# The end of batch 1's attention: masks of the last head pair on TensorE, its heads in one run, x of two pairs transposed by DMA, an earlier Gelu table load

## Chip, cores and metric

The kernel runs on 1 core of one Trainium2 chip. The time is the device time of one execution in microseconds; the figure for a kernel is the median of its runs.

## The reference

Attention with a forget gate over 8 batches and 8 heads, 576 tokens, head size 64, followed by a two-layer network with an exact Gelu on all 4608 tokens:

```
scores = q @ k.T / sqrt(64);  cum = cumsum(log(clip(f, 1e-4, 1)))
attn   = softmax(where(causal, scores + cum[i] - cum[j]))
x      = (attn @ v) with heads side by side: [4608, 512]
out    = gelu(x @ w_in) @ w_out          # w_in 512x2048, w_out 2048x512
```

All inputs and the output are float32; the kernel multiplies in bf16.

## The kernel before, in words

The work goes batch by batch, in an order that is written out by hand (`tc.manual_schedule()`): each engine executes its instructions in the order in which the code issues them. The engines are called PE (TensorE), DVE (VectorE), ACT (ScalarE), POOL (GpSimd) and SP (SyncE, which issues DMAs).

The 8 heads of a batch are 4 pairs. For a pair `i`, `scores(b, i, t)` (L280) computes one of four tiles `t` of transposed scores for both heads into PSUM (pool `s_psum`, two buffers), keys on the partitions and queries along the free dimension; ACT takes the exp into `e` (L310). Only blocks on or below the diagonal are computed. The diagonal blocks need the causal mask, and this is done in one of two ways: where `on_pe` is true (L281), PE adds a large negative number by small matmuls of the constants `key_of` and `after` ahead of the exp; elsewhere POOL sets the forbidden entries of `e` to zero by `affine_select` behind the exp (L312). Per pair there are five such diagonal blocks.

`attend` (L324) multiplies e with the weighted v (`vw`, the factor of the forget gate and a column of sums in it) into the PSUM tile `o` (pool `o_psum`, two buffers); `normalize` (L339) has DVE take the reciprocal of the sums and write x (bf16, tag `x`, three buffers). x has tokens on the partitions; the first GEMM wants it transposed, as xT. There are two ways for that too: `to_xT` (L357) transposes on PE through PSUM and copies by DVE or ACT, and `x_dma` (L369) has SP issue one DMA that transposes through the DMA crossbar. Batches 2 to 7 use `x_dma`, batches 0 and 1 `to_xT`.

Then `gemm1` (L381) makes 16 blocks of the hidden layer for the first 512 tokens of the batch (the last 64 are gathered in `tails` for one pass at the end), and ACT's Gelu follows each (L406). The second GEMM of a batch is used as filler: it is a generator from which `take(fill, n)` takes n matmuls in the gaps of the next batch's attention. For batch 1 the filler is `gemm2_first` (L510), half of batch 0's second GEMM: 16 matmuls of 128x512 at L518, into two buffers of `m_psum`, which DVE copies out at the 12th step and ACT at the 16th (L530).

`second_attention` (L721) is batch 1. Its order for the pairs: `tiles(i, t)` issues two score tiles, `run(i)` attends to and normalizes both heads of a pair. At the end come the transposes of x of pairs 0 and 1 by PE (`o_psum` buffers, DVE copies), pair 2 (into `s_psum`, ACT copy), and pair 3 inside `gemm1_begin` (L642), which starts the first GEMM with two blocks on the parts of x that are there (`m_psum`, the two buffers that the filler leaves). Between them SP issues `transpose_dma(2, ...)` (L226), the crossbar transposes of q and k of batch 2, as soon as POOL's loads of them have landed, and after that `load_v(2)`. DVE sorts the transposed q and k in `untangle` (L241). POOL waits for k (`behind`, L570) and issues two loads of w_out.

ACT keeps one table of functions at a time; a change between Exp and Gelu shows as ACT_TABLE_LOAD. A copy runs with either. A tiny activation on `warm` (L735) loads Exp's table ahead of batch 1's attention.

Of the kernel before, what the change touches and what calls it, by code (L numbers as in the profile page):

```python
# [11 lines left out]
Act = mybir.ActivationFunctionType  # L12
# [7 lines left out]
HP = 4  # L20
# [33 lines left out]
def kernel(  # L54
# [10 lines left out]
    nc = tc.nc  # L65
# [24 lines left out]
    o_psum = ctx.enter_context(tc.tile_pool(name="o_psum", bufs=2, space=PSUM))  # L90
# [40 lines left out]
    warm = consts.tile([P, TC], BF16)  # L131
# [42 lines left out]
    def load_w_out(c):  # L174
        kt = slice(c * n_ff // 4, (c + 1) * n_ff // 4)
        nc.gpsimd.dma_start(w_out_sb[:, kt, :], w_out_r[:, kt, :])
# [82 lines left out]
    def vw(b):  # L259
        if b not in vw_of:  # L260
            vw_of[b] = v_pool.tile([P, H, NBLK, D + 1], BF16, tag="vw", name=f"vw{b}")
        return vw_of[b]

    def weigh_v(b, i, eng=nc.gpsimd):

        hs = slice(2 * i, 2 * i + 2)
        bh = b * H + 2 * i
        w = wT[:, :, bh : bh + 2].rearrange("p n h -> p h n")
        eng.tensor_tensor(  # L269
            vw(b)[:, hs, :, 0:D],  # L270
            v_sb[:, hs, :, :],
            w.unsqueeze(3).to_broadcast([P, 2, NBLK, D]),
            Alu.mult,
        )
        if b:
            eng.tensor_copy(vw(b)[:, hs, :, D], w)
# [1 line left out]
    e_of = {}  # L278

    def scores(b, i, t):  # L280
        on_pe = b == 0 or (b == 1 and i == 0)  # L281
        st = s_psum.tile([P, 2, 512], FP32, tag="s", name=f"s{t}")
        c = 0
        for n, q0, w in STILES[t]:
            z = D if n == NBLK - 1 else 0
            masked = on_pe and c in SDIAG[t]
            for half in range(-1, 2 if masked else 0):
                if half == 0 and z:
                    continue
                for h in range(2):  # L290
                    d = slice(h * D, (h + 1) * D)
                    if half < 0:
                        to = st[:, h, c + z : c + w]
                        ab = kT[i][d, K0[n] : K0[n] + P], qT[i][d, q0 + z : q0 + w]
                    else:
                        last = (half + 1) * D
                        to = st[:, h, c + z : c + last]
                        c0 = (1 + h - half) * D
                        ab = key_of[d, c0 : c0 + P], after[d, c0 + z : c0 + last]
                    nc.tensor.matmul(  # L300
                        to, *ab, start=half < 0, stop=half == 1 or not masked
                    )
            c += w
        z = D if t == 1 else 0
        if z:
            et = e4[(b * HP + i) % len(e4)]
        else:
            et = e_pool.tile([P, 2, 512], BF16, tag=f"e{t}", name=f"e{t}")
        e_of[b, i, t] = et
        nc.scalar.activation(et[:, :, z:c], st[:, :, z:c], Act.Exp, scale=scale)  # L310
        for c0 in [] if on_pe else SDIAG[t]:
            nc.gpsimd.affine_select(  # L312
                out=et[:, :, c0 + z : c0 + P],
                in_=et[:, :, c0 + z : c0 + P],
                compare_op=Alu.is_ge,
                fill=0.0,
                base=z,
                pattern=[[0, 2], [1, P - z]],
                channel_multiplier=-1,
            )  # L320
# [3 lines left out]
    def attend(b, i, h, ms):  # L324
        if (b, i, h) not in o_of:
            o_of[b, i, h] = o_psum.tile([P, NBLK, D + 1], FP32, tag="o", name="o")
        o = o_of[b, i, h]
        for m in ms:
            for n in range(m + 1):
                t, c = where(n, m)  # L330
                nc.tensor.matmul(  # L331
                    o[:, m, :],
                    e_of[b, i, t][:, h, c : c + P],
                    vw_of[b][:, 2 * i + h, n, :],
                    start=(n == 0),
                    stop=(n == m),
                )

    def normalize(b, i, h):  # L339
        if (b, i) not in x_of:  # L340
            x_of[b, i] = x_pool.tile([P, NBLK, 2, D], BF16, tag="x", name="x")
        o = o_of[b, i, h]
        r = x_pool.tile([P, NBLK], FP32, tag="r", name="r")
        nc.vector.reciprocal(r, o[:, :, D])  # L344
        nc.vector.tensor_tensor(  # L345
            x_of[b, i][:, :, h, :],
            o[:, :, 0:D],
            r.unsqueeze(2).to_broadcast([P, NBLK, D]),
            Alu.mult,
        )  # L350

    def xT(b):
        if b not in xT_of:
            xT_of[b] = xT_pool.tile([P, n_dm, XC], BF16, tag="xT", name="xT")
        return xT_of[b]

    def to_xT(b, i, copy, pool=m_psum, tag="m", ps=None):  # L357
        if ps is None:
            shape = [P, 2, 1024] if pool is s_psum else [P, XC]
            ps = pool.tile(shape, BF16, tag=tag, name="ps_x")  # L360
            if pool is s_psum:
                ps = ps[:, 0, 0:XC]
        for m in range(NBLK):
            nc.tensor.transpose(  # L364
                ps[:, m * P : (m + 1) * P], x_of[b, i][:, m, :, :], ident_bf
            )
        copy(xT(b)[:, i, :], ps)

    def x_dma(b, i):  # L369
        nc.sync.dma_start_transpose(  # L370
            xT(b)[:, i, :].rearrange("d (m p) -> d m p", p=P),
            x_of[b, i].rearrange("p m h d -> p (m h d)"),
        )
# [136 lines left out]
    def gemm2_first(c):  # L510

        pss = [
            m_psum.tile([P, d_model], FP32, tag="m", name="ps2") for _ in range(2)
        ]
        for kq in (0, 4):
            for ts in range(2):
                for kt in range(kq, kq + 4):
                    nc.tensor.matmul(  # L518
                        pss[ts],
                        g_of[c][kt][:, ts * P : (ts + 1) * P],  # L520
                        w_out_sb[:, kt, :],
                        start=(kt == 0),
                        stop=(kt == 7),
                    )
                    if kt == 7:
                        ot_of.append(
                            o_pool.tile([P, d_model], FP32, tag="ot", name="ot")
                        )
                        copy = nc.scalar.copy if ts else nc.vector.tensor_copy
                        copy(ot_of[ts], pss[ts])  # L530
                    yield
# [27 lines left out]
    def take(gen, n):  # L559
        for _ in range(n):  # L560
            if next(gen, "end") == "end":
                return
# [7 lines left out]
    def behind(t, h):  # L570

        g = x_pool.tile([P, 1], FP32, tag="gate", name="gate")
        nc.gpsimd.tensor_copy(g[:PT], t[:, h, 0:1])
# [147 lines left out]
    def second_attention():  # L721


        b, fill = 1, gemm2_first(0)

        def av(i, h):
            attend(b, i, h, (0, 1, 2, 3, 4))
            normalize(b, i, h)

        def transposes(i, pool, tag):  # L730
            for which in range(2):
                transposes_first(b, i, which, pool, tag)


        nc.scalar.activation(warm[0:1, 0:1], warm[0:1, 0:1], Act.Exp)  # L735
        def tiles(i, t):
            scores(b, i, t)
            scores(b, i, t + 1)

        def run(i):  # L740
            av(i, 0)
            av(i, 1)

        tiles(0, 0)
        transposes(1, o_psum, "o")
        transposes(2, m_psum, "m")
        transposes(3, o_psum, "o")
        tiles(0, 2)
        take(fill, 2)
        tiles(1, 0)  # L750
        run(0)
        tiles(1, 2)
        take(fill, 4)
        weigh_v(1, 2)
        tiles(2, 0)
        run(1)
        weigh_v(1, 3)
        tiles(2, 2)
        take(fill, 4)
        tiles(3, 0)  # L760
        transpose_dma(2, 0, 4)
        transpose_dma(2, 4, 8)
        to_xT(b, 0, nc.vector.tensor_copy, o_psum, "o")
        to_xT(b, 1, nc.vector.tensor_copy, o_psum, "o")
        take(fill, 2)
        tiles(3, 2)
        behind(qk_of[2][1], H - 1)
        load_w_out(2)
        load_w_out(3)
        run(2)  # L770
        take(fill, 4)
        av(3, 0)
        both = s_psum.tile([P, 2, 1024], BF16, tag="s", name="ps_x2")
        to_xT(b, 2, nc.scalar.copy, ps=both[:, 0, 0:XC])
        av(3, 1)
        gemm1_begin(1, both)
        x_tail(1)
        load_v(2)
# [67 lines left out]
```

## Time and profile before

| what | value |
|---|---|
| median of 10 runs | 338.18 us (337.06 to 340.92) |
| the profiled execution, its own time | 337.12 us |
| its span in the profile | 335.3 us |
| granted TensorE clock, mean | 0.998 |
| exp (L310) | 128 activations, 100.2 us |
| POOL select (L312) | 135, 49.1 us, mean 383 ns |
| transposes of x on PE (L364) | 40, first at 21.2, last at 56.7 us |
| DMA, x to xT (L370) | 24, first at 84.0 us |

Times in the profile are microseconds from the start of the span. A timeline row gives the start, the time until the end of the last instruction merged into the row, the engine, the line of the kernel, the operation with its operands (written <- read), how many were merged, and in brackets the idle time ahead of it with what ended it. Matmuls are pipelined: the next starts before the last one's end, so the difference of starts is what one takes of PE. A few per cent of the matmul records are missing.

### The profile page before, as it was taken

The page shows a single profiled execution, that of the slowest core. Times are in us where ns is not written, and L with a number is a line of the kernel's source. Part 1 is how long each engine was busy: PE and PEld are TensorE (multiplying, and loading weights), DVE is VectorE, ACT ScalarE, POOL GpSimd, SP SyncE. Part 2 cuts the span into 40 slices and gives each one's busy share as a digit, 9 for nine tenths or more (in the row PEclk, how much of TensorE's full clock was granted, in tenths as well). Part 3 has the DMA queues.
Part 4 walks back from the last instruction along what each step waited for, and adds up shares of the span by engine and source line. Part 5 has one row for each costly group of instructions (what it writes and reads, how often), then busy time and mean ns, then how long its engine had stood idle before and what let it go on. Part 6 is the DMA issues. An engine that isn't in the chain of part 4 may idle for free.

```text
span 335.3 us, 7780 instructions
## 1 busy us (share of the span) xinstructions
PE 323.0 (96%) x3121; PEld 171.5 (51%) x3161; DVE 181.2 (54%) x414; ACT 209.3 (62%) x299; POOL 121.4 (36%) x250
## 2 busy tenths in 40 slices
PE   8799989999999999999999999999999999999995
PEld 3574556445554456445644555446544654444443
DVE  4770456674358945894579547964696550020011
ACT  6977797773634787378827892787378846404600
POOL 8280296037436144713445343624351420000000
PEclk9999999999999999999999999999999999999999
DMA  7999999979998999599947888689700241011013
GB/s 115 187 169 193 210 185 147 203 144 148 183 219 177 142 199 188 102 140 153 226 113 112 167 178 175 92 146 201 162 31 2 85 64 59 0 66 62 0 40 85
DMA packets 104627, 44.16 MB, mean 132 GB/s; under 512 B 83408, under 2 KB 100048, under 8 KB 104592
## 3 DMA queue, kind: packets, MB, share of 16 engines
q1 hardware_dynamic: 87296, 29.52, 46.7%
q0 software_dynamic: 16896, 13.63, 27.4%
q8 instruction: 24, 0.39, 0.5%
q10 hardware_dynamic: 400, 0.52, 0.4%
q14 instruction: 11, 0.09, 0.1%
HBM read 36.85 MB, written 9.44 MB: 138 GB/s over the span
## 4 chain that ended last, share of the span: by engine, by line
PE 90%; issue 2%; SPq 2%; DVE 1%; POOL 1%; ACT 1%; DMA 1%; POOLq 0%; ACTq 0%
PE ps L386 36%; PE ps L482 26%; PE o L331 10%; PE ps L422 8%; PE s L300 7%; SPq L120 2%; ACT e L310 1%; PE ps L542 1%; DMA v_sb<-in_v_dram 1%; POOL q L108 1%; PE ps_x L364 1%; PE ps L518 0%; POOL k L108 0%; DVE qT L217 0%; DVE kT L217 0%
## 5 line engine op out<-in xcount | busy, mean ns | idle before, releaser
L406 ACT ACTIVATE g<-ps 128x512 bf16<-128x512 f32 x144 | 82.1, 601 | 83.8 <-PE ps L386 83.8
L310 ACT ACTIVATE e<-s 128x896 bf16<-128x896 f32 (+2 forms) x128 | 100.2, 835 | 20.7 <-PE s L300 17.8
L386 PE MATMUL ps<-xT,w_in_sb 128*128 128x512 bf16 x497 | 111.7, 379 | 0.8
L482 PE MATMUL ps<-w_out_sb,g 64*128 64x512 bf16 (+1 forms) x692 | 104.4, 376 | 1.6 <-issue 1.3
L386 PEld LDWEIGHTS <-w_in_sb 128*128 128x128 bf16 x576 | 55.9, 98 | 67.7 <-issue 2.1
L312 POOL TENSOR_SCALAR_AFFINE_SELECT e<-e 128x256 bf16<-128x256 bf16 (+1 forms) x135 | 49.1, 383 | 84.7 <-ACT e L310 84.3
L482 PEld LDWEIGHTS <-g 64*128 64x128 bf16 (+1 forms) x711 | 39.4, 95 | 34.7 <-issue 4.2
L269 POOL TENSOR_TENSOR vw<-v_sb,wT 128x640 bf16<-128x640 f32 x30 | 38.6, 1289 | 27.3 <-PE s L300 14.3
L300 PE MATMUL s<-qT,kT 64*128 64x320 bf16 (+4 forms) x384 | 43.8, 276 | 2.8 <-ACT e L310 1.6
L250 DVE COPY kT<-tk 64x288 bf16<-64x288 bf16 x96 | 43.0, 448 | 1.6
L250 DVE COPY qT<-tq 64x288 bf16<-64x288 bf16 x96 | 39.8, 414 | 4.1 <-DMA tq<-q 2.7
L490 DVE COPY ot<-ps 128x512 f32<-128x512 f32 x20 | 13.8, 691 | 47.1 <-PE ps L482 47.1
L331 PEld LDWEIGHTS <-e 128*128 128x128 bf16 x960 | 34.5, 98 | 8.6 <-POOL e L312 2.5
L331 PE MATMUL o<-vw,e 128*128 128x65 bf16 x960 | 37.4, 194 | 1.3 <-issue 0.8
L345 DVE TENSOR_TENSOR x<-o,r 128x320 bf16<-128x320 f32 x64 | 31.4, 491 | 3.0 <-DMA xT<-x 0.8
L431 DVE COPY ot<-ps 128x512 f32<-128x512 f32 (+2 forms) x9 | 5.7, 632 | 49.6 <-PE ps L422 49.6
L300 PEld LDWEIGHTS <-kT 64*128 64x128 bf16 x384 | 19.8, 94 | 24.4 <-issue 7.9
L422 PE MATMUL ps<-w_out_sb,g 128*128 128x512 bf16 (+2 forms) x142 | 27.9, 355 | 0.1
L422 PEld LDWEIGHTS <-g 128*128 128x128 bf16 x144 | 13.5, 98 | 14.5
L344 DVE RECIPROCAL r<-o 128x5 f32<-128x5 f32 x64 | 12.1, 188 | 12.1 <-PE o L331 12.0
L502 DVE TENSOR_TENSOR ot<-ot,ps 128x512 f32<-128x512 f32 x22 | 15.1, 684 | 1.1
L386 PE MATMUL ps<-tails,w_in_sb 128*128 128x512 bf16 x63 | 14.2, 377 | 0.1
(69 smaller groups left out, 136.6 us busy)
## 6 DMA issues: line engine op xcount, KB each, us to landing
out_dram<-ot SPq DMA_DIRECT2D x32, 256.0 KB, 2.5
v_sb<-in_v_dram SPq DMA_DIRECT2D x24, 256.0 KB, 4.9
q<-in_q_dram POOLq DMA_DIRECT2D x6, 576.0 KB, 6.4
k<-in_k_dram POOLq DMA_DIRECT2D x6, 576.0 KB, 8.3
v_sb<-in_v_dram SPq DMA_DIRECT2D x22, 128.0 KB, 5.0
w_in_sb<-in_moe_w_in_dram POOLq DMA_DIRECT2D x4, 512.0 KB, 8.1
w_out_sb<-in_moe_w_out_dram POOLq DMA_DIRECT2D x4, 512.0 KB, 9.0
q<-in_q_dram POOLq DMA_DIRECT2D x4, 144.0 KB, 4.6
```

The source lines that it names most:

```text
L250: nc.vector.tensor_copy(rows[:, odd], src[odd * D : (odd + 1) * D, 2 * i + h].rearrange("d j p -> d p j"),)
L269: eng.tensor_tensor(vw(b)[:, hs, :, 0:D], v_sb[:, hs, :, :], w.unsqueeze(3).to_broadcast([P, 2, NBLK, D]), Alu.mult,)
L300: nc.tensor.matmul(to, *ab, start=half < 0, stop=half == 1 or not masked)
L310: nc.scalar.activation(et[:, :, z:c], st[:, :, z:c], Act.Exp, scale=scale)
L312: nc.gpsimd.affine_select(out=et[:, :, c0 + z : c0 + P], in_=et[:, :, c0 + z : c0 + P], compare_op=Alu.is_ge, fill=0.0, base=z, pattern=[[ ...
L331: nc.tensor.matmul(o[:, m, :], e_of[b, i, t][:, h, c : c + P], vw_of[b][:, 2 * i + h, n, :], start=(n == 0), stop=(n == m),)
L345: nc.vector.tensor_tensor(x_of[b, i][:, :, h, :], o[:, :, 0:D], r.unsqueeze(2).to_broadcast([P, NBLK, D]), Alu.mult,)
L386: nc.tensor.matmul(ps, w_in_sb[:, kt, ffb * P : (ffb + 1) * P], src[:, kt, 0:TC], start=(kt == 0), stop=(kt == n_dm - 1),)
L406: nc.scalar.activation(g_of[c][ffb], ps, Act.Gelu)
L422: nc.tensor.matmul(pss[ts][:, c0:c1], g_of[c][kt][:, ts * P : (ts + 1) * P], w_out_sb[:, kt, c0:c1], start=(kt == 0), stop=(kt == n_ff - 1),)
L482: nc.tensor.matmul(banks[r], g_of[c][kt][rows, ts * P : (ts + 1) * P], w_out_sb[rows, kt, :], start=kt == (steps.index("r") if r else 0), ...
L502: nc.vector.tensor_tensor(ot, ot, bank, Alu.add)
```

## The change

Four edits, all in batch 1. `scores` masks pair 3 (`HP - 1`) on PE as it does pair 0. x of pairs 0 and 1 goes to xT by `x_dma` right behind its `run`, in place of two `to_xT`. The two heads of pair 3 are issued in one `run(3)`, and the PE transposes of pair 2 follow it, where they lay between its heads; of the filler's last six matmuls four come ahead of the last two score tiles and two behind `run(2)`, where it was two and four. A tiny Gelu on `warm` is issued behind the last exp.

```diff
     def scores(b, i, t):
-        on_pe = b == 0 or (b == 1 and i == 0)
+        on_pe = b == 0 or (b == 1 and i in (0, HP - 1))
...
         run(0)
+        x_dma(b, 0)
         tiles(1, 2)
...
         run(1)
+        x_dma(b, 1)
         weigh_v(1, 3)
...
         transpose_dma(2, 0, 4)
         transpose_dma(2, 4, 8)
-        to_xT(b, 0, nc.vector.tensor_copy, o_psum, "o")
-        to_xT(b, 1, nc.vector.tensor_copy, o_psum, "o")
-        take(fill, 2)
+        take(fill, 4)
         tiles(3, 2)
+        nc.scalar.activation(warm[0:1, 0:1], warm[0:1, 0:1], Act.Gelu)
         behind(qk_of[2][1], H - 1)
         load_w_out(2)
         load_w_out(3)
         run(2)
-        take(fill, 4)
-        av(3, 0)
+        take(fill, 2)
+        run(3)
         both = s_psum.tile([P, 2, 1024], BF16, tag="s", name="ps_x2")
         to_xT(b, 2, nc.scalar.copy, ps=both[:, 0, 0:XC])
-        av(3, 1)
         gemm1_begin(1, both)
```

## The prediction

> **What bounds the kernel now.** I read the page's busy shares first, then the chain of work that ended last, then the timelines of PE, ACT, DVE, POOL and SP between 36 and 76 us, where batch 1's attention and what follows it lie, and last the rows of the DMA issues. The shares and the chain by engine:
>
> ```profile
> PE 323.0 (96%) x3121; PEld 171.5 (51%) x3161; DVE 181.2 (54%) x414; ACT 209.3 (62%) x299; POOL 121.4 (36%) x250
> PE 90%; issue 2%; SPq 2%; DVE 1%; POOL 1%; ACT 1%; DMA 1%; POOLq 0%; ACTq 0%
> ```
>
> PE is on the chain for 90% of the span, and from 57.44 us, where batch 1's first GEMM runs freely, the chain is PE nearly without a break. So the question is narrow: when does PE get to the matmul after the last `to_xT` of batch 1 (56.79 us now), and does anything later go late. PE around the change:
>
> ```profile
> 50.09 0.69 PE L300 MATMUL s<-qT,kT 64*128 64x256 bf16 x8
> 50.71 0.73 PE L364 MATMUL ps_x<-key_of,x 128*128 128x128 bf16 x10
> 51.28 0.59 PE L518 MATMUL ps<-w_out_sb,g 128*128 128x512 bf16 x2
> 51.80 0.74 PE L300 MATMUL s<-qT,kT 64*128 64x448 bf16 x4
> 52.47 1.12 PE L331 MATMUL o<-vw,e 128*128 128x65 bf16 x30
> 53.65 0.81 PE L518 MATMUL ps<-w_out_sb,g 128*128 128x512 bf16 x3
> 54.30 0.64 PE L331 MATMUL o<-vw,e 128*128 128x65 bf16 x15
> 54.77 0.44 PE L364 MATMUL ps_x<-key_of,x 128*128 128x128 bf16 x5
> 55.05 0.64 PE L331 MATMUL o<-vw,e 128*128 128x65 bf16 x15
> 55.53 1.02 PE L386 MATMUL ps<-xT,w_in_sb 128*128 128x512 bf16 x4
> 56.50 0.45 PE L364 MATMUL ps_x<-key_of,x 128*128 128x128 bf16 x5
> ```
>
> The reader is to use the starts: a duration contains about 0.16 us of pipeline that overlaps the next start. Ten transposes take 51.28 - 50.71 = 0.57 us of PE, five take 0.28, one fill matmul 0.215, a head of attention 0.48. One record of the fill is missing (16 weight loads, 13 matmuls over the stage), it lies at 53.43. PE stands still only near 50.3, 52.1 and 56.4, some 0.4 us together. ACT and SP beside it:
>
> ```profile
> 50.56 3.22 ACT L310 ACTIVATE e<-s 128x896 bf16<-128x896 f32 x4 [0.18 <-PE s L300]
> 54.50 0.58 ACT L530 COPY ot<-ps 128x512 f32<-128x512 f32 x1 [0.72 <-PE ps L518]
> 55.25 0.69 ACT L367 COPY xT<-ps_x 128x640 bf16<-128x640 bf16 x1 [0.17 <-PE ps_x L364]
> 55.96 1.28 ACT L406 ACT_TABLE_LOAD   x1
> 58.07 1.09 ACT L406 ACTIVATE g<-ps 128x512 bf16<-128x512 f32 x2 [0.83 <-PE ps L386]
> ```
>
> ```profile
> 50.91 1.41 SPq L236 DMA_TRANSPOSE tq<-q  x1
> 53.67 1.29 SPq L236 DMA_TRANSPOSE tk<-k  x1
> 55.01 2.33 SPq L236 DMA_TRANSPOSE tq<-q  x1
> 57.40 4.87 SPq L236 DMA_TRANSPOSE tk<-k  x1
> 62.36 4.09 SPq L120 DMA_DIRECT2D v_sb<-in_v_dram  x3
> ```
>
> Two things to see: after the table load ACT still waited 0.83 us for PE, so that load holds nobody up; and SP is free from 41.84 to 50.91.
>
> **The change, part by part.**
>
> *Masks by PE.* Pair 3 adds 18 small matmuls. Pair 0 of this batch shows their price:
>
> ```profile
> 38.67 0.25 PE L300 MATMUL s<-after,key_of 64*128 64x64 bf16 x4
> 38.76 0.25 PE L300 MATMUL s<-qT,kT 64*128 64x192 bf16 x2
> 42.08 0.26 PE L300 MATMUL s<-after,key_of 64*128 64x64 bf16 x4
> 42.27 0.39 PE L518 MATMUL ps<-w_out_sb,g 128*128 128x512 bf16 x1
> ```
>
> A group of four takes 0.09 us (38.67 to 38.76) up to 0.19 (42.08 to 42.27). Four groups and a pair of 0.02: between 0.4 and 0.8 us; I take 0.4, since the two groups inside a tile are the clean ones. Part of it hides: tile (3,1) waits until 50.44 for the exp of (2,3) anyhow, and tile (3,3) until 52.23 for the exp of (3,1). But the first tile's 0.17 us come before its exp, which had itself waited for PE (the 0.18 in brackets), so the four exps move from 50.56 to about 50.75.
>
> *Selects off POOL.* Five of 0.29 to 0.41 us go. The last ends at 54.26; PE needs its tile at 54.30, behind the fill. So this covers about itself: worth 0 now. But with only two fills after `run(2)`, the select would have held PE some 0.2 us; that is why the edits belong together. POOL also reaches the wait for k and the two w_out DMAs sooner, at k's landing.
>
> *Transposes of pairs 0 and 1.* PE is relieved of 0.57 us, DVE of two copies (0.89 us in all), which no one awaited closely. The bank order of the o pool changes: its two buffers go straight from pair 1 to pair 2.
>
> *Two x DMAs on SP.* They are issued when x is normalized, at 45.98 and 49.38 us, behind v loads whose issue ended at 41.84. SP's issue of one is 1.2 to 2.2 us (24 of them later), so the second ends at 50.6 to 51.6; the q transpose queued behind waited for its q data until 50.91, so it loses 0 to 0.7 us. Landing of an x DMA is 2.6 us at the least, 2.8 in the middle and 6.2 at most; the 6.2 is the one at 84.0 us, which ran under a bulk load of q and k, as these will. Lands: pair 0 by 52.2, pair 1 between 52.0 and 55.6. The first GEMM reads pair 1 in its second matmul, at about 55.8. Cost 0, just. Another reader of that landing: `normalize(3,0)` reuses x's first buffer and needs pair 0's DMA done by about 54.9; it has 2.7 us. A rule of the Trainium skill speaks to this ("DMA: Bandwidth & Descriptors", Queues, rings and completion order): an engine takes turns between queue rows, a packet at a time. A lone x DMA at 264 us used 0.82 us of all 16 engines and landed in 2.6; an even share with the software queue gives an estimate of 2.6 + 0.8 = 3.4 us. By the rule pair 1 lands at 52.8, by the worst row at 55.6; I take the row as the bound, and no stall by either.
>
> *What the DMAs delay.* The engines are full from 44 to 56.4 us, nearly idle from 56.5 to 57.5, full again to 71. Two x DMAs add 2 x 0.82 = 1.6 us; that gap takes up about 1.0. So the transposed q of heads 4 to 7, which DVE awaits until 65.66, comes 0.6 us later (0 to 1.6). DVE's untangling then ends at 71.7 instead of 71.06. Next for DVE is the sum at 72.07 (which waits 1.00 us for PE now), and the bank that it frees is wanted at 73.94, free at 73.48: slack 1.4 us in all. v lands near 72.3 for POOL's weighing; the selects that follow end at 78.4 and are read at 81.45, slack 3 us. Cost 0; at the bad end 0.2 us, or 0.8 if the gap absorbs nothing and SP also loses its 0.7.
>
> *Heads in one run, fill moved.* No matmul is added: two fills move ahead of tile (3,2), two stay between `run(2)` and `run(3)`. The cover between the heads of pair 2 and 3 shrinks from 0.87 us of fill to 0.43, and the five transposes between the heads of pair 3 go behind them. The o pool has two buffers, so head (3,1) needs (2,1) normalized. That was done at 54.50; here it moves with `run(2)`. Walk: exp (3,0) 50.75; four fills to 51.6; tile (3,2) at 51.7; exp (3,1) ends 52.38, tile (3,3) at 52.42; `run(2)` at 52.8 (was 52.47); fills from 53.75 to 54.2; (2,0) normalized 54.2, head (3,0) at 54.2 to 54.7; (2,1) normalized 54.8, head (3,1) at 54.85 to 55.35, a stall of 0.15; transposes of pair 2 to 55.6; first GEMM block to 56.5; its second `to_xT` at 56.5 (x of (3,1) is ready at 56.3), and 56.8 at the matmul after. Before it was 56.79: **0.0 us**. In a sum: -0.57 of transposes, +0.4 of masks, +0.15 on the o buffers.
>
> *Gelu's table sooner.* The load moves ahead of two ACT copies, behind the last exp at about 53.97. The tiny activation costs 0.11 to the next (40.20 to 40.31). The copy that frees the second m bank then runs 55.37 to 55.96, and PE asks for that bank at 56.04; the copy of pair 2 ends 56.65, asked for at 56.8. Both margins are 0.1 us, where 0.9 and 1.0 were before: a loss of 0 to 0.3 if ACT is a little later. Nothing is gained, since the Gelu waited for PE. The rule against it is the skill's "ScalarE: Activation LUTs", What ACT_TABLE_LOAD costs: 1283 ns and a drain of 1380 for each switch. The first number is the row's. A drain would push both copies by 1.38 us, and PE by about 1.3. The trace speaks against: the load at 38.91 begins within 0.03 us of the last Gelu's end (38.29 + 0.60) and the next activation starts at 40.20, 1.28 later plus 0.01. I take 1.28.
>
> **Sum.** Path 0.0 us, side costs nearer 0 than their ends. The profiled execution has a span of 335.3 us, 337.12 in its own time, so 1.8 lie around the span; the median of the ten runs is 338.18, 1.06 above that execution. I keep the difference and move the median by 0.0: 338.2 us.
>
> **The rivals.** A measurement of this kernel can tell about 0.5% (1.7 us) from no change.
> - *Even* (chance 0.62): as walked, 338.2, within 0.5 us.
> - *A small gain* (0.14): the masks hide fully in the waits at 50.44 and 52.23, and the o stall doesn't appear. Then -0.57, 337.6. For it: PE does stand there. Against: ACT's row of four exps starts later, and sets 52.23.
> - *A small loss* (0.13): masks at 0.8, ACT's copies late by 0.3, DVE late by 0.8: together up to +1.5, 339.7; typically +0.8, 339.0.
> - *The x DMA becomes the wait* (0.08), the other side: pair 1's x lands late and PE stands before the first GEMM. Decisive from a landing of 6.3 us, slower by the bound from 8.0. The transposed q issued at 55.01 took 10.6 us in a like crowd; that landing would put it at 60.0 and cost 4.2 us, 342.4. For it: the queue is full of q and k until 53.7. Against: the larger q transpose issued at 50.91, in the same crowd, took 3.9.
> - *Gain over the bound* (0.03): nothing on the path is that long (0.57 us of work and 0.4 of standing still); only the scatter of runs.
>
> Range: 337.2 (the small gain and 0.4 for scatter of medians) to 339.5 (most of the small loss). Chances with a share for scatter: faster 0.05, same 0.85, slower 0.10.
>
> **What would show it.** Right: 18 more masks in 50 to 53 us; no waits on xT's DMA at L386; two SP transposes at 46 and 49.4; the table load at about 54; Gelu still waiting for PE; the chain PE from 57 us. Wrong: PE idle before L386 released by a DMA or by the ACT copy of `ot`; DVE's untangling past 72.5; a start of the free-running GEMM more than 0.5 us off 57.4.

## The result, and the profile after

The changed kernel takes 339.69 us (median of 14 runs, 338.16 to 342.10), the kernel before 337.91 us in the runs beside it: ratio 1.0053, 95% interval 1.0033 to 1.0073. That is 1.8 us slower, outside the range of the prediction. The profiled execution took 339.49 us with a span of 337.2 us.

To see where, I cut each span at four points of PE's timeline that every kernel has: A, the first score matmul of batch 1's pair 3; B, the first matmul behind the last `to_xT` of batch 1; C, the first matmul of `gemm2_second` (L542); D, the first matmul of batch 2's first head (L331); E, the end.

| kernel | A | B - A | C - B | D - C | E - D | span |
|---|---|---|---|---|---|---|
| before | 50.09 | 6.70 | 13.35 | 11.31 | 253.85 | 335.3 |
| after | 50.43 | 7.89 | 13.35 | 12.01 | 253.52 | 337.2 |

Up to A the work is the same but for the two x DMAs, and from D it is the same; the differences of +0.34 and -0.33 are about as large as those among the kernels below that have no x DMA, and I take them as scatter. The loss lies in two places: 1.19 us between A and B, 0.70 us between C and D, together 1.9. The first lies in PE's timeline of the kernel after (to be held against the rows from 55.53 on before, which the prediction shows):

```profile
55.65 0.44 PE L364 MATMUL ps_x<-key_of,x 128*128 128x128 bf16 x5
56.81 1.29 PE L386 MATMUL ps<-xT,w_in_sb 128*128 128x512 bf16 x4 [0.72 <-DMA xT<-x]
58.03 0.45 PE L364 MATMUL ps_x<-key_of,x 128*128 128x128 bf16 x5
```

The transposes of pair 2 end near 55.93; the first GEMM then stands for pair 0's x DMA until 56.81, and its four matmuls take 1.22 us where they took 0.97 before: the second of them starts only at 57.29, when pair 1's x has come (57.2). The second place is in DVE's timeline, first a row of before, then four of after:

```profile
65.66 1.34 DVE L250 COPY qT<-tq 64x288 bf16<-64x288 bf16 x4 [2.66 <-DMA tq<-q]
```

```profile
56.86 0.49 DVE L345 TENSOR_TENSOR x<-o,r 128x320 bf16<-128x320 f32 x1 [1.44 <-DMA xT<-x]
69.28 1.35 DVE L250 COPY qT<-tq 64x288 bf16<-64x288 bf16 x4 [3.07 <-DMA tq<-q]
74.72 0.69 DVE L550 TENSOR_TENSOR ot<-ot,ps 128x512 f32<-128x512 f32 x1
75.44 0.69 DVE L502 TENSOR_TENSOR ot<-ot,ps 128x512 f32<-128x512 f32 x1
```

The first row of after is the x buffer that pair 0's DMA still has to read. In its second, the transposed q of heads 4 to 7 comes at 69.28 instead of 65.66, untangling ends at 74.7 instead of 71.1, and the sums that free the o bank follow without a gap, and PE takes the bank at 76.18 (before: 73.94, without a wait):

```profile
73.94 1.89 PE L482 MATMUL ps<-w_out_sb,g 64*128 64x512 bf16 x16
```

```profile
76.18 1.88 PE L482 MATMUL ps<-w_out_sb,g 64*128 64x512 bf16 x15 [0.33 <-DVE ot L502]
```

The chain of work that ended last, in order of time, tells the same story for the kernel after; before, it held ACT's exps and PE up to 53.65 us, and PE alone from there to the end of this stretch:

```profile
44.67 12.14 DMA k<-in_k_dram
56.83 1.40 SPq L236
58.28 10.97 DMA tq<-q
...
75.44 0.70 DVE ot L502
76.18 3.66 PE ps L482 x31
```

The load of batch 2's k took 12.14 us (9.3 before, 9.9 to 10.5 in those kernels below that have no DMA of x here), SP's transposes waited for it, and the transpose of q issued at 58.28 took 11 us.

### The profile page after: what moved, and what is told of

Its sections match the earlier page's. It is cut to its first block, busy times and chain, and to the rows that moved or that the text cites. A ratio compares the mean times of both kernels' runs of the same rounds, so it can differ in the third digit from the quotient of the medians.

```text
span 337.2 us, 7796 instructions
## 1 busy us (share of the span) xinstructions
PE 323.3 (96%) x3129; PEld 171.6 (51%) x3169; DVE 180.3 (53%) x412; ACT 209.4 (62%) x300; POOL 120.3 (36%) x245
## 4 chain that ended last, share of the span: by engine, by line
PE 82%; DMA 8%; DVE 3%; POOL 3%; SPq 2%; issue 2%; ACT 0%; POOLq 0%; ACTq 0%
PE ps L386 32%; PE ps L482 26%; PE o L331 9%; PE ps L422 8%; PE s L300 6%; DMA k<-in_k_dram 4%; DMA tq<-q 3%; SPq L120 2%; DMA v_sb<-in_v_dram 1%; POOL q L108 1%; DVE qT L250 1%; DVE kT L250 1%; POOL vw L269 1%; POOL k L108 0%; SPq L236 0%
## 5 line engine op out<-in xcount | busy, mean ns | idle before, releaser
L312 POOL TENSOR_SCALAR_AFFINE_SELECT e<-e 128x256 bf16<-128x256 bf16 (+1 forms) x130 | 47.3, 384 | 85.9 <-ACT e L310 85.8
L482 PEld LDWEIGHTS <-g 64*128 64x128 bf16 (+1 forms) x711 | 40.3, 95 | 35.0 <-issue 4.8
L331 PE MATMUL o<-vw,e 128*128 128x65 bf16 x960 | 37.4, 194 | 1.8 <-DVE vw L269 1.1
L331 PEld LDWEIGHTS <-e 128*128 128x128 bf16 x960 | 34.4, 98 | 9.3 <-POOL e L312 2.5
```

Source lines behind the costliest of these rows:

```text
L312: nc.gpsimd.affine_select(out=et[:, :, c0 + z : c0 + P], in_=et[:, :, c0 + z : c0 + P], compare_op=Alu.is_ge, fill=0.0, base=z, pattern=[[ ...
L331: nc.tensor.matmul(o[:, m, :], e_of[b, i, t][:, h, c : c + P], vw_of[b][:, 2 * i + h, n, :], start=(n == 0), stop=(n == m),)
L482: nc.tensor.matmul(banks[r], g_of[c][kt][rows, ts * P : (ts + 1) * P], w_out_sb[rows, kt, :], start=kt == (steps.index("r") if r else 0), ...
```

## The experiments

My theory (T1): the two x DMAs, on SP's hardware queue, hardly move while POOL's bulk loads of q and k of batch 2 are in flight, and land when those end. Rivals: the rest of the change costs the time (R1); the x buffer on DVE carries it (R3); the crossbar is slow in this place whatever else moves (R2). Each kernel's profiled execution is one run, and so are the times of e6, e11 and e12.

**The x DMAs alone, and everything but them.** e1 is before with `x_dma(b, 0)` and `x_dma(b, 1)` in place of the two `to_xT`. e2 is after with this undone:

```diff
         run(0)
-        x_dma(b, 0)
...
         run(1)
-        x_dma(b, 1)
...
+        to_xT(b, 0, nc.vector.tensor_copy, o_psum, "o")
+        to_xT(b, 1, nc.vector.tensor_copy, o_psum, "o")
         take(fill, 4)
```

> Before, with one edit of the change alone: x of pairs 0 and 1 by x_dma behind their runs, no PE transposes for them. Theory (T1: the crossbar DMAs starve behind POOL's bulk loads of q and k of batch 2 until those end, so x lands near 56.7 us): landing of 7 to 10 us, DVE's normalize of head (3,0) and the first GEMM wait for DMA xT<-x, PE's second to_xT block of gemm1_begin about 1 us later than before, DVE's untangling past 73 us; time 1.0 to 2.0 us over before, ratio 1.003 to 1.006. Rival R1 (the rest of the change, masks, one run and table load, costs the time): landing may be long, but the time stays within 0.5 us of before, ratio 0.999 to 1.001.

> After, with PE's transposes of pairs 0 and 1 put back where they were and no x_dma; masks, one run of heads, moved fills and the early table load stay. T1: back at before or a little over (PE has 0.4 us more masks and no saving): ratio 0.999 to 1.002, no wait for DMA at L386 or L345. R1: slower by 1.0 to 2.0 us, ratio 1.003 to 1.006, with PE standing at the o buffers or at the ACT copy of ot.

**The DMAs without a reader.** e3 is e2 with two DMAs of the same x into a tile that nobody reads, and five x buffers:

```diff
+    dead = consts.tile([P, 2, XC], BF16, name="dead")
+
+    def dead_dma(i):
+        nc.sync.dma_start_transpose(
+            dead[:, i, :].rearrange("d (m p) -> d m p", p=P),
+            x_of[1, i].rearrange("p m h d -> p (m h d)"),
+        )
```

> As the kernel without x_dma, and in addition two crossbar DMAs of the same x at the same two places into a tile that nobody reads, with five x buffers so that nobody waits for them; nothing of the output depends on them. It measures what the DMAs do to other transfers alone. If the direct waits carry the loss (T1a): within 0.5 us of the kernel without x_dma, though k and the transposed q land 1 to 3 us later. If delayed transfers carry it (T1b: DVE's untangling and the o bank behind it): 1 us or more over the kernel without x_dma.

**The load out of the way.** e4 moves `load_qk_tokens(2)` from batch 0's GEMM to behind `weigh_v(1, 3)`:

> After, with POOL's load of q and k of batch 2 issued only behind weigh_v of pair 3 (about 51 us) in place of before batch 1's scores (43.6 us), so that the two x DMAs run before it. T1: the x DMAs land in 2.6 to 4 us, no wait at L386 and L345; PE's first GEMM starts about 1.2 us sooner than in after; the transposed q and k come some 5 us later, which costs 0 to 4 us at DVE's untangling. A contention of the crossbar with anything else (R2: the DMAs are slow by themselves here, with w_out and v alone in flight): landing stays over 6 us.

| kernel | ratio to before, interval | A | B - A | C - B | D - C | E - D | span |
|---|---|---|---|---|---|---|---|
| e1 | 1.0029 (1.0009 to 1.0049) | 50.51 | 8.23 | 13.35 | 12.24 | 253.57 | 337.9 |
| e2 | 1.0009 (0.9986 to 1.0032) | 50.15 | 7.14 | 13.35 | 11.31 | 253.85 | 335.8 |
| e3 | 1.0015 (0.9991 to 1.0038) | 50.94 | 7.14 | 13.35 | 12.58 | 253.99 | 338.0 |
| e4 | 1.0233 (1.0196 to 1.0270) | 53.58 | 7.25 | 13.34 | 18.45 | 253.48 | 346.1 |

e1 shows both losses of the changed kernel, 1.53 and 0.93 us in its trace, with no other edit made; e2 shows neither wait, but 0.44 us of its own between A and B. The waits of e1 for x, in PE's and DVE's timelines:

```profile
57.23 0.38 PE L386 MATMUL ps<-xT,w_in_sb 128*128 128x512 bf16 x1 [1.12 <-DMA xT<-x]
57.28 0.49 DVE L345 TENSOR_TENSOR x<-o,r 128x320 bf16<-128x320 f32 x1 [1.69 <-DMA xT<-x]
```

By times alone, e1 is slower than before and e2 can't be told from before, but their intervals overlap, and e7 below, which has no x DMA either, is as far over before as e1 (1.0026 against 1.0029). So the times do not separate T1 from R1; what does is the trace. e3 has nobody waiting for the dead DMAs, so A to B is e2's 7.14; yet C to D is 12.58: the second loss needs only that the DMAs are there. They push k to 12.0 us (10.2 in e2) and everything that hangs on it. So the two losses have one source and two ways: a wait for x, and transfers that come late (the waiting behind it is T1b). e3's time rose by less than its trace (1.0015), so how often the second loss falls in full is not settled.

e4 answers what the DMAs are slow with. The DMA view of the kernel after, for issues between 48 and 52 us (queue, q0 POOL's and q1 SP's: packets, MB, the time that the packets took as a share of 16 engines, which can add up to more than 100%; then issue: count and median landing in us):

```profile
q0 software_dynamic: 786, 0.59, 111.9%
q1 hardware_dynamic: 85, 0.02, 4.1%
...
xT<-x SPq DMA_TRANSPOSE x2, 9.0
```

and the same for e4, where q and k are not yet issued and the last w_out load is through at 49.1, just after the first x DMA is issued at 49.01:

```profile
xT<-x SPq DMA_TRANSPOSE x1, 2.7
```

In those four microseconds the hardware queue, with up to 1344 packets of x to move (672 for one x DMA), got 85 packets and the software queue 786. That is no even sharing, but it does not stay so. From 48 to 51 us the hardware queue got none (e8, where pair 0's x DMA was issued at 46.11, has none from 46 to 50, beside 774 of the load). Its next packets came between 51 and 52, and from 52 to 54 the two queues took turns one for one in the kernel after:

```profile
q0 software_dynamic: 370, 0.28, 90.4%
q1 hardware_dynamic: 367, 0.09, 37.2%
```

They are even in e10 as well, for the transpose of q beside k's load (330 against 332 from 56 to 58 us). So x lost its time in the first 4 to 5 us behind its issue and then shared packet by packet with what was left of k. Why it was kept out at first, no run here shows.

The landings over the kernels, each against the moment at which the bulk load in flight is through (the start of the transpose on SP that waits for it):

| kernel | pair 0's x DMA: issued, landing | lands at | the load is through |
|---|---|---|---|
| after | 46.33, 10.4 us | 56.8 | k, 56.8 |
| e1 | 46.25, 10.9 us | 57.2 | k, 57.2 |
| e3 (dead) | 46.44, 10.7 us | 57.2 | k, 57.2 |
| e5 | 48.78, 8.0 us | 56.8 | k, 56.6 |
| e9 | 45.79, 9.5 us | 55.3 | k, 55.2 |
| e8 | 46.11, 8.6 us | 54.7 | q, 53.8 (k issued at 51.5, through at 58.5) |
| e10 | 47.70, 6.8 us | 54.5 | q, 53.2 (k issued at 53.1, through at 61.0) |
| e4 | 49.01, 2.7 us | 51.7 | none of q and k in flight |

The load that counts is the one issued ahead of the x DMA: in e8 and e10 (both below) x lands 3.8 and 6.5 us before k, issued behind it, is through. R2 falls by e4. But e4 pays 9 us, its q and k come too late for DVE's untangling: C to D is 18.45, PE standing at the o bank for `ot` of L550 (3.8 us) and then going on at a lower clock (0.79 and 0.50 from 82 to 86 us). Another 3.5 us of its trace lie ahead of A, of which 1.95 are a wait of PE for a w_out load; their cause was not looked for.

**One load later, one wait less.** e5 is after with `x` in five buffers (`bufs=3` to `bufs=5`). e8 is after with only k moved (`which="q"` at the old place, `which="k"` behind `weigh_v(1, 3)`). e6 is e3 with a plain `dma_start` in place of the transposing one.

> After, with five x buffers in place of three, so that normalize of head (3,0) no longer waits for pair 0's x DMA to have read its buffer (1.44 us in after). T1: that wait goes, but the first GEMM still waits for xT of pairs 0 and 1 until about 57.2 us, so the PE transposes of pair 3 start at most 0.1 us sooner: time as after within noise, ratio to before 1.003 to 1.006. R3 (the buffer wait on DVE carries the loss): 0.7 us or more is gained back, ratio at most 1.003, with PE's wait for DMA xT<-x at most what it was.

> After, with only the k half of batch 2's bulk load moved behind weigh_v of pair 3 (about 51 us); q stays at 43.6 us. T1: pair 0's x DMA (46.3 us) lands when q has, near 49 to 51 us, pair 1's (49.7 us) within 3 to 4 us; no wait at L386 or L345; PE's transposes of pair 3 about 1.3 us sooner than in after; k lands near 57 us, not later than the 56.8 of after, so DVE's untangling stays near 74 us and costs 0.3 to 0.7 us: ratio to before 0.999 to 1.003. R2 (the crossbar is slow in this place whatever POOL loads): x lands at 56 us again.

> As the kernel with the two dead crossbar DMAs, but plain copies of the same bytes on the same queue at the same two places; nobody reads them. It tells whether it is the hardware queue that is held up by POOL's bulk loads (T1q: landing 6 us or more here too) or the crossbar transpose alone (T1x: landing 2 to 4 us). One look; only the landings are read, and k's.

| kernel | ratio to before, interval | A | B - A | C - B | D - C | E - D | span |
|---|---|---|---|---|---|---|---|
| e5 | 1.0016 (0.9982 to 1.0050) | 52.87 | 6.72 | 13.34 | 11.31 | 253.46 | 337.7 |
| e8 | 1.0154 (1.0114 to 1.0195) | 50.46 | 6.71 | 13.35 | 16.70 | 253.48 | 340.7 |
| e6 | one run, 337.91 us | 50.31 | 7.15 | 13.34 | 11.39 | 253.81 | 336.0 |

e5 did not decide what it was made for: in its profiled execution A came 2.4 us later and k's load only 0.7 (issued at 45.34), so that x was there in time and nobody waited at all. R3 is left open by it, but the trace of after bounds it: PE's four matmuls, which wait for x themselves, are done near 57.94, and the transposes of pair 3, which need the heads that DVE held back, start at 58.03. The buffer wait alone cost some 0.1 us. e5 shows two other things: how far the loss hangs on where k's load happens to fall against the attention, and, with e8, that the rest of the changed path takes 6.72 and 6.71 us when x is in time, against 6.70 before.

In e8 pair 0's DMA waited for q's load, which was through at 53.8 and not at 49 to 51 as I expected, and then had its turn; x was not waited for, and A to B is level with before. The price came back at the o bank, 5.4 us where I expected at most 0.7: k through at 58.5, the transposed q of heads 4 to 7 at 71.1. PE's timeline of e8, and PE's granted clock in the row of windows behind it (window, length, busy time and instructions of PE, PEld, DVE, ACT and POOL, clock, DMA share, GB/s):

```profile
77.31 0.37 PE L482 MATMUL ps<-w_out_sb,g 64*128 64x512 bf16 x1 [2.82 <-DVE ot L550]
```

```profile
78.00:80.00 2.00, 1.97 (x16) 1.04 (x17) 1.26 (x2) 0.00 (x0) 1.29 (x2) 0.81 0.36 133
80.00:82.00 2.00, 2.00 (x14) 1.00 (x11) 0.00 (x0) 0.70 (x1) 2.00 (x4) 0.50 0.35 131
```

A stand of about 3 us cost the stand and then some 2 us more, while the clock was at 0.81, at 0.50 and, from 82 to 84 us, at 0.83.

e6: plain copies took 6.8 and 5.7 us, the crossbar's 10.7 and 7.9 in e3. So the hardware queue is held up with a plain copy too, and in these two traces the transposing DMA longer; the second copy missed my bound of 6 by 0.3. The copy goes in larger packets (0.14 MB in 117 of them from 50 to 52 us, against 0.09 MB in 367 above) and so needs fewer turns; whether that is the reason was not tested. No plain copy ran without a load in flight.

**The rest of the change.** e7 is e2 without the early Gelu; e11 is e7 with the masks of pair 3 on POOL as before; e12 is before with only `on_pe` changed.

> The kernel without x_dma, and without the early Gelu as well: masks, run(3) and the moved fills are all that is left of the change. The early table load holds the ACT copy of ot until 56.38 us in the kernel without x_dma, where PE could take the bank at 56.23. T1: the second block of the first GEMM starts 0.2 us sooner, the table load is behind the xT copy again and still ends before Gelu is due; time 0.2 us less than without x_dma, ratio 0.998 to 1.001 to before. Rival (the load was worth something early): time 0.3 us or more over the kernel without x_dma.

> Before, with only the heads of pair 3 in one run and the fills moved: no masks on PE for pair 3, no x_dma, no early Gelu. The distance from pair 3's first score to the GEMM behind the last to_xT is read: 6.70 us in before, 6.87 with the masks on PE. My walk (the select would hold PE some 0.2 us with only two fills behind run(2), the masks cost 0.4 less what hides): 6.6 to 6.9. If the masks are hidden: 6.87 or more, with PE waiting for POOL's select at L331.

> Before, with only the masks of pair 3 on PE. The same distance is read: 6.70 in before; by my walk (0.4 of masks, 0.1 hidden behind the exp of the pair before, no wait for POOL to save) 6.9 to 7.1; if they hide fully 6.70.

| kernel | time | B - A | C - B | D - C |
|---|---|---|---|---|
| e7 | ratio 1.0026 (1.0005 to 1.0047) | 6.87 | 13.35 | 11.31 |
| e11 | one run, 338.42 us | 6.80 | 13.34 | 11.33 |
| e12 | one run, 338.03 us | 6.95 | 13.34 | 11.32 |

Masks alone cost 0.25 us, one run of heads alone 0.10, both 0.17 (the masks then save a wait for POOL's select of 0.2, which e11 shows at L331); e11 and e12 fell where I expected them. The early table load costs 0.27: that is e2's 7.14 less e7's 6.87. In e2 PE's and ACT's timelines show it:

```profile
55.80 1.23 PE L386 MATMUL ps<-xT,w_in_sb 128*128 128x512 bf16 x4
```

```profile
54.42 1.28 ACT L767 ACT_TABLE_LOAD   x1
55.71 0.20 ACT L767 ACTIVATE warm<-warm 1x1 bf16<-1x1 bf16 x1
55.82 0.56 ACT L530 COPY ot<-ps 128x512 f32<-128x512 f32 x1
```

The copy of `ot` comes out of the table load's way at 56.38, so the second block, whose bank it frees, starts at 56.43 instead of 56.23, and the four matmuls with their gap take 1.22. e7's ratio missed what I expected: it is no faster than e2 by the times. Differences of 0.3 us are below what these runs resolve, and I rest the split on the traces.

**Later w_out.** The transposed q waited for in the kernel after was in flight beside POOL's last w_out loads, so the same hold-up could stand behind the 0.70 at the o bank (T2). e9 is after, and e10 is e8, with this:

```diff
-        behind(qk_of[2][1], H - 1)
-        load_w_out(2)
-        load_w_out(3)
         run(2)
...
         x_tail(1)
+        behind(qk_of[2][1], H - 1)
+        load_w_out(2)
+        load_w_out(3)
```

> After, with POOL's two last loads of w_out (and the wait for k ahead of them) moved behind the copy of x's tail, so that they are issued near 59.5 us in place of 57.1, and the transposed q of heads 4 to 7 (issued at 58.3) has a start of some 2 us on them. T2 (the 0.70 us that PE loses at the o bank at 76 us come from the transposed q landing only when the w_out load ends): q of heads 4 to 7 lands at 62 to 66 us in place of 69.3, DVE's untangling ends before 73.5, no wait for DVE ot at L482; the distance from the first L542 matmul to batch 2's first head is 11.3 us as in before, not 12.0. The wait for x stays: 7.7 to 8.2 us from pair 3's first score to the GEMM behind the last to_xT. Time about 0.7 less than after, ratio to before 1.001 to 1.005. Rival (the 0.7 come with v or DVE's own order): 12.0 stays.

> The kernel with k late, with the w_out loads behind the tail copy as well. T1 and T2 together: no wait for x (6.7 us from pair 3's first score to the GEMM, as in before), the transposed q of heads 4 to 7 at 64 to 68 us in place of 71.1, so that the o bank costs 0 to 1 us in place of the 5.4 lost with k late; ratio to before 0.999 to 1.005. This is the version with the best chance to be level with before or ahead. Rival (the load of k, two transposes late, delays DVE anyhow): the o bank still costs 2 us or more.

e9: ratio 1.0049 (1.0027 to 1.0072), no gain; A to B 6.86 us, C to D 13.11. The wait for x, which I expected to stay (7.7 to 8.2 us), was nearly gone in its trace: k's load was through at 55.2 already (56.8 in after). The edit acts only behind that, so the first loss is not the same in every execution. e10: 1.0179 (1.0135 to 1.0223), far over what I expected, 6.85 and 17.81. DVE's timeline of e9 shows what happened:

```profile
63.98 1.34 DVE L250 COPY qT<-tq 64x288 bf16<-64x288 bf16 x4
70.29 1.33 DVE L250 COPY kT<-tk 64x288 bf16<-64x288 bf16 x4 [4.96 <-DMA tk<-k]
```

The q of heads 4 to 7, issued at 56.50, landed in 4.1 us, before the w_out load (issued at 58.15) got going, where it took 11.0 in after: this trace, too, has the hold-up come from a load issued ahead. But the k of these heads, issued at 58.48 behind the load, took 11.8 us, and the wait went over to it. The stall was moved, not removed. In e10 k is through only at 61.0, so both transposes fall behind the load. A later place for w_out that lets all four out first was not tried; its data are needed at C.

No version that I ran beats the kernel before.

## Why the prediction was wrong, step by step

- **The path of PE: right, to 0.02 us.** The walk gave a net of 0.0 between A and B; with x in time, e5 and e8 have 6.72 and 6.71 against 6.70. Its steps hold too: counted from A, `run(2)` begins at 2.64 us in e8 (2.7 in the walk), the transposes of pair 2 at 5.22 (5.26), the second `to_xT` at 6.44 (6.4). The sum that closes it is another matter: it counts PE's work as time, and is right because two terms are too large by about the same. Masks and one run were put at 0.4 + 0.15; together they cost 0.17 (e7). The removed transposes were put at -0.57; they bring 0.16, from e7's 6.87 to e8's 6.71, in part because PE then waits for the exp of an earlier tile, as the walk had it (e8):

```profile
52.77 0.31 PE L300 MATMUL s<-qT,kT 64*128 64x320 bf16 x2 [0.23 <-ACT e L310]
```

- **Early Gelu: right in size, in its range.** 0 to 0.3 was put down and 0 taken. It is 0.27 where PE transposes pairs 0 and 1, and nothing in e8, where ACT's exps are earlier. The drain that the prediction set aside is not seen in after either: the load begins at 54.15 and the next activation at 55.44, 1.29 later.
- **The step that failed: the landing of the x DMAs.** "By the rule pair 1 lands at 52.8, by the worst row at 55.6; I take the row as the bound, and no stall by either." Pair 0 landed at 56.8 (10.4 us) and pair 1 at 57.2 (7.5), and PE stood. A landing in a crowd was read as a duration that travels with the operation. In these traces it ended with the loads issued ahead of it or with it. The profile of before held this: the x DMA issued at 84.0 landed at 90.2, and the load of k issued at 75.9 took 14.0 us, to 89.9; the transposed q issued at 55.0 ended at 65.6, beside the second w_out load, issued a tenth behind it at 55.1 and through at 65.3 (10.1 us; 7.9 for the first). I had named the second as a rival's price and set against it the 3.9 us of the transpose issued at 50.91, which was short since k's load ended at 53.7. The estimate from the Trainium skill's taking of turns ("DMA: Bandwidth & Descriptors", Queues, rings and completion order), 3.4 us, fails too. The turns themselves are in the trace, 367 packets against 370 from 52 to 54 us; the estimate let them begin with the issue, and there were none from 48 to 51.
- **What the DMAs delay: right in kind, too small.** 1.6 us of DMA work, of which an idle gap at 56.5 to 57.5 would take up 1.0, 0.6 us on the transposed q. It was 3.6 us (69.28 against 65.66). The gap was gone, filled by the transposes that k had pushed back (952 packets of SP's queue from 56.8 to 58 us); and w_out, which waits for k, was issued at 57.10 instead of 54.33, so that q's second transpose ran beside it. The slack of 1.4 us at the o bank was right in size and was used up: PE itself came to C 1.5 us later (71.67 against 70.14), the slack took 1.4 of the 2.1 that remained, and 0.7 reached PE. The other traces fit this sum. This q lands 4.5 us ahead of C in before and in e5, 3.0 in e6, 2.4 in after, 2.2 in e1 and 1.8 in e3, and C to D is 0, 0.08, 0.70, 0.93 and 1.27 us over before: nothing is lost down to about 3.1 us ahead of C, and from there what comes later is lost in full.
- **The rivals.** The fourth case, "the x DMA becomes the wait", named the place and the mark (landing over 6.3 us) and had 0.08. It gave 4.2 us for a landing as late as 60.0; x came at 57.3.

## What to carry to other kernels

The landing time of a DMA in a busy stretch is no property of that DMA: look up which loads were issued ahead of it or together with it and when they ended, and take that moment, for the new transfer at its new place. Work taken off the bound engine and given to a DMA is a gain only if the data comes in time; here 0.57 us of PE's work, worth 0.16 us of time, were traded for a wait of 1.2, and 0.7 through transfers that others needed. And a stall at a handover with 1.4 us of slack is decided by a chain of loads (q, k, then w_out and the transposes): shift one and ask each that waits behind it.

## What the runs showed of the hardware

- A transposing DMA on SP's hardware queue, issued while POOL's software queue had bulk loads in flight, moved nothing at first (in after 0 packets against 383 from 48 to 50 us), then took turns with the load one packet for one (367 against 370 from 52 to 54), and landed within about 1.4 us of the end of the loads issued ahead of it: 6.8 to 10.9 us for pair 0's x in seven kernels, against 2.7 in e4 without q and k. Plain copies of the same bytes beside such loads took 6.8 and 5.7.
- After PE stood for about 3 us in e8 the granted clock was 0.81, 0.50 and 0.83 in the next three stretches of two microseconds; the shorter stands of the kernel after, up to 0.9 us, left it at 1.00.
